# Decay rows of the first four blocks: small TensorE products and copies in place of a trip through DRAM

## The chip, the cores and the metric

One Trainium2 chip, one NeuronCore. The metric is the device time of one launch in microseconds. The kernel before has been run three times: 526.5, 527.76 and 527.88 us, median 527.76 us. One execution was also recorded by the hardware profiler; every duration below comes from that record, whose times count from the start of its span.

## What is computed

A gated linear recurrence over 768 steps (4 batches, 8 heads of 48), whose output goes through a feed-forward layer with a squared ReLU. q, k, v and alpha are float32; the two weight matrices arrive as 64-bit floats and are converted to float32 on the chip.

```python
def _attn_ref(q, k, v, alpha):
    for t in range(S):
        state = alpha[:, :, t, :, None] * state + einsum('bhd,bhe->bhde', k[:, :, t], v[:, :, t])
        y[:, :, t] = einsum('bhd,bhde->bhe', q[:, :, t], state)
...
h = np.maximum(x @ w_in, 0.0)      # x: 3072 x 384, w_in: 384 x 2048
return (h * h @ w_out)             # w_out: 2048 x 384
```

## The kernel before

The sequence is cut into chunks of 128 steps. A block is one chunk of one batch (all 8 heads), so there are 24 blocks, numbered chunk first: blocks 0 to 3 are the first chunk of the four batches. Four blocks make a group, whose 512 tokens go through the feed-forward layer together, so there are six groups.

For each block, `ln` takes the logarithm of alpha (L258), `cs` sums it along the chunk by one product with a triangular matrix (L280), and `eb` and `ei` make from the sums the decay `b` and its inverse `inv`, 128 steps by 384 (L291, L295). `mq` and `mk` scale q and k with them (L299). `qT` and `kT` turn q and k on TensorE (L336), `qc` and `kc` copy them to SBUF (L352). `sc` makes the scores and `kv` the sums of k times v in the same two PSUM banks (L399, L427); `am` masks the scores (L410); `us` adds the old state to the first half of kv (L440); `st` makes the next state: the second half of kv is added (L456) and the sum is scaled by the block's total decay (L457). `ya` and `yb` make the output of two blocks at once (L379, with a no-op on GpSimd between the two, L496), `ev` copies it into the layer's input `x` (L594).

The total decay is the last row of `b`, 384 numbers. L457 needs it as `last`, turned so that head and feature lie on the partitions: feature d of head 2p + e on partition 64 e + d, column p. Before, `bl` (L313) stores the row to DRAM (L317) and `br` (L319) loads it back in the turned layout with two DMAs of 192 numbers (L327). All DMAs are issued by SyncE in order. `st` runs for all but the last chunk, so 20 blocks need a `last`.

The tile `b` has two buffers, so block 3's `b` is written where block 0's stood once that has been read for `last`. All PSUM tiles share eight banks.

What runs before TensorE gets into the feed-forward layer is written out by hand: the word list `AT['first']` (L19) is walked at L948, and each word appends its step's instructions to the in-order queues of the engines. It holds everything for blocks 0 to 3, the words `ha0` to `ha3` and `hb0` to `hb3` (products of the feed-forward layer's first weights with the first half, blocks 0 and 1, and the second half of the group's tokens: L896, with ReLU and square on ScalarE, L902 and L905), and the conversion of the first three pieces of the 64-bit weights. One piece is converted by `first` on VectorE (L163, L167), `middle` on ScalarE (L177, L180) and `second` on VectorE (L188, L192, L195). `zeros` (L365) are products of zeros whose result nobody reads. What comes later (the other weights' conversion, the attention blocks 4 to 23) is woven into the feed-forward products by due times (`PLAN`, `EARLY`, `weave`), with `bl` and `br` for each of blocks 4 to 19.

The steps around the change run, by the word list, in this order:

```
... us0 bl1 qc1 kT1 ... br1 ei2 us1 ya0 eb2 yb0 zeros2 ln3 zeros2 mk2 load3k mq2 kT2 ev0 qT2 kc2 bl0 cs3
second0 qc2 eb3 first1 sc2 load3q kv2 ei3 mk3 load4q bl2 mq3 middle1 ha0 qT3 qc3 kT3 am2 kc3 weights6 second1
ha1 sc3 us2 load4k weights1 br2 br0 kv3 st0 bl3 ha2 am3 us3 load4v first2 ya2 weights3 br3 yb2 st3 ev2 middle2
ha3 hb3 second2 weights5 st2 hb0 weights4 load4a hb1 st1 hb2
```

Each engine takes only its own part of a word, so on VectorE us3 comes behind am3, that behind st0, and first2 behind us3.

## Time and profile before

| what | value |
|---|---|
| median of three runs | 527.76 us (526.5 to 527.88) |
| the profiled execution: its span, from the first to the last instruction (the page gives no other time of it) | 525.7 us |
| TensorE busy | 510.9 us, 97% of the span |
| VectorE busy | 363.8 us, 69% |
| ScalarE busy | 313.7 us, 60% |
| row stores (L317) | 20 of 1.5 KB, 0.24 to 0.78 us of issue each |
| loads of `last` (L327) | 40 of 0.8 KB, 0.33 to 2.80 us of issue each |
| waits for `last` (L457) | 8.6 us in 4 of 20 instructions |

A line of a timeline gives start, length, engine, line of the code, operation, output<-inputs, shapes and count, and in brackets the idle time of the engine ahead of it with what ended it. "PE y L379 <- DVE us L440: 4.0, 1, 4.0" in a list of waits reads: TensorE at L379 waited for VectorE's L440, 4.0 us in total, once, longest 4.0. The row PEclk of the page gives the TensorE clock that was granted in each of 40 slices of the span, in tenths.

### The profile page before, as it was taken

What the parts mean: (1) busy time and instruction counts of PE and PEld (TensorE: products, weight loads), DVE (VectorE), ACT (ScalarE), POOL (GpSimd) and SP (SyncE); (2) the same over time, 40 slices, a digit from 0 to 9 for tenths busy, and PEclk for the clock granted to TensorE, in tenths of its full rate; (3) what the DMA queues carried; (4) which work ended last, traced back from release to release, by engine and by line L of the source; (5) the groups of instructions that cost most, each with busy time, mean ns of one, the idle gap of its engine ahead of it and who ended that gap; (6) DMA issues with size and microseconds to landing.
All of it is one profiled execution on the core that took longest, in us unless ns stands there. A gap on an engine that the chain in (4) does not pass through costs nothing.

```text
span 525.7 us, 12899 instructions
## 1 busy us (share of the span) xinstructions
PE 510.9 (97%) x5276; PEld 421.6 (80%) x5276; DVE 363.8 (69%) x631; ACT 313.7 (60%) x654; POOL 5.3 (1%) x29
## 2 busy tenths in 40 slices
PE   6969999999999999999999999999999999999997
PEld 5656446567888769888899988899988899988997
DVE  4757978899879687865698365697365485363861
ACT  4638986588798576466963266963265773164620
POOL 4000000000000000000000000000000000000000
PEclk9888999999999999999999999999999999999999
DMA  9996877445488667898975697865774454798201
GB/s 190 191 262 137 237 200 200 106 93 211 153 235 232 151 192 188 246 357 225 252 189 187 218 281 183 214 175 175 224 251 150 153 156 138 240 362 287 87 0 60
DMA packets 140994, 102.34 MB, mean 195 GB/s; under 512 B 111476, under 2 KB 114568, under 8 KB 140936
## 3 DMA queue, kind: packets, MB, share of 16 engines
q1 hardware_dynamic: 140936, 101.53, 68.8%
q8 instruction: 41, 0.67, 0.6%
q14 instruction: 17, 0.14, 0.1%
HBM read 84.18 MB, written 17.33 MB: 193 GB/s over the span
## 4 chain that ended last, share of the span: by engine, by line
PE 76%; DVE 9%; ACT 7%; DMA 4%; issue 2%; SPq 2%; DVEq 0%; POOLq 0%
PE h L703 32%; PE o L786 32%; PE y L379 4%; ACT power L177 2%; PE T L556 2%; PE h L896 2%; PE sckv L399 2%; PE sckv L427 1%; SPq L119 1%; DVE w_out L192 1%; DVE w_out L195 1%; DMA wd<-do 1%; DMA v_in<-in_v_dram 1%; DVE wl L626 1%; DMA last<-row 1%
## 5 line engine op out<-in xcount | busy, mean ns | idle before, releaser
L703 PE MATMUL h<-xa,wb 128*128 128x512 f32 x240 | 68.8, 395 | 0.0
L703 PE MATMUL h<-xl,wl 128*128 128x512 f32 x240 | 67.8, 391 | 0.0
L703 PE MATMUL h<-xd,wd 128*128 128x512 f32 x240 | 66.6, 392 | 0.0
L594 ACT COPY x<-y 32x256 f32<-32x256 f32 (+2 forms) x132 | 47.3, 365 | 23.1 <-PE y L379 12.8
L720 ACT ACTIVATE h<-h 128x512 f32<-128x512 f32 x40 | 23.3, 581 | 59.9 <-PE h L703 59.7
L626 DVE TENSOR_TENSOR hid<-h,hid 128x512 f32<-128x512 f32 x40 | 27.5, 688 | 41.5 <-PE h L703 38.8
L786 PE MATMUL o<-wd,hd 128*128 128x384 f32 x304 | 54.4, 335 | 1.4 <-DVE osb L823 1.0
L786 PEld LDWEIGHTS o<-wd,hd 128*128 128x128 f32 x304 | 52.7, 188 | 2.4 <-DVE osb L823 1.4
L786 PE MATMUL o<-wb,ha 128*128 128x384 f32 x160 | 54.1, 338 | 0.0
L786 PE MATMUL o<-w_out,hid 128*128 128x384 f32 x160 | 53.5, 490 | 0.0
L786 PE MATMUL o<-wl,hl 128*128 128x384 f32 x160 | 53.5, 334 | 0.0
L703 PEld LDWEIGHTS h<-xl,wl 128*128 128x128 f32 x240 | 45.0, 188 | 10.0 <-DVE xl L626 0.3
L703 PEld LDWEIGHTS h<-xd,wd 128*128 128x128 f32 x240 | 44.6, 188 | 9.1
L703 PEld LDWEIGHTS h<-xa,wb 128*128 128x128 f32 x240 | 44.3, 188 | 9.2
L786 PE MATMUL o<-wb,hx 128*128 128x384 f32 x144 | 48.7, 338 | 0.0
L786 PE MATMUL o<-wl,hx 128*128 128x384 f32 x144 | 48.1, 334 | 0.0
L786 PEld LDWEIGHTS o<-w_out,hid 128*128 128x128 f32 x160 | 29.9, 190 | 19.7
L896 PE MATMUL h<-x,w_in 128*128 128x512 f32 (+1 forms) x120 | 44.8, 528 | 0.1
L676 ACT ACTIVATE ha<-hid 128x512 fp32r<-128x512 f32 x40 | 25.5, 636 | 23.8 <-DVE hx L626 13.0
L718 ACT ACTIVATE hid<-h 128x512 f32<-128x512 f32 x40 | 24.3, 607 | 25.2 <-PE h L703 25.1
L896 PEld LDWEIGHTS h<-x,w_in 128*128 128x128 f32 x120 | 23.7, 201 | 17.7 <-issue 14.4
L626 DVE TENSOR_TENSOR hl<-hid,ha 128x512 fp32r<-128x512 f32 x40 | 27.4, 685 | 11.6 <-ACT ha L676 11.6
(114 smaller groups left out, 878.3 us busy)
## 6 DMA issues: line engine op xcount, KB each, us to landing
wd<-do SPq DMA_DIRECT2D x36, 384.0 KB
wl<-lo SPq DMA_DIRECT2D x34, 384.0 KB
wl<-li SPq DMA_DIRECT2D x32, 384.0 KB
wd<-di SPq DMA_DIRECT2D x32, 384.0 KB
raw<-in_moe_w_in_dram SPq DMA_DIRECT2D x8, 768.0 KB
raw<-in_moe_w_out_dram SPq DMA_DIRECT2D x8, 768.0 KB
v_in<-in_v_dram SPq DMA_DIRECT2D x24, 192.0 KB
out_dram<-osb SPq DMA_DIRECT2D x24, 192.0 KB
```

The lines of the kernel that those rows point to most:

```text
L177: nc.scalar.activation(out=power, in_=power, func=AF.Relu, scale=2.0**23, bias=rebias)
L379: ins = nc.tensor.matmul(out=ys[e][64 * half : 64 * half + D + G * e, m % 2, p // 2, t], lhsT=lhsT, rhs=rhs, start=(half, e) not in seen, ...
L399: nc.tensor.matmul(out=ps[e][HALF[h], 0, p, :], lhsT=ks[rows, p, HALF[h]], rhs=qs[rows, p, HALF[h]], start=True, stop=True, skip_group_che ...
L556: nc.tensor.transpose(out=ps[h][:, i, p, :], in_=rows[HALF[h], 128 * p : 128 * (p + 1)], identity=ident[HALF[h], HALF[h]],)
L594: copy(out=x[kk][to : to + m, t : t + 2], in_=blk[n]["y"][e][r : r + m, :, p // 2],)
L626: nc.vector.tensor_tensor(out=o, in0=x, in1=z, op=op)
L676: nc.scalar.activation(out=a, in_=x, func=AF.Copy, scale=NEAR)
L703: nc.tensor.matmul(out=acc["h", j], lhsT=here[w, "i", p][:, kk, jj * 128 : (jj + 1) * 128], rhs=x_parts[x][:, kk], start=start and kk == 0 ...
L718: nc.scalar.activation(out=hid[j], in_=x, func=AF.Copy, scale=E)
L720: nc.scalar.activation(out=x, in_=x, func=AF.Copy, scale=1.0 + E)
L786: nc.tensor.matmul(out=acc[t][:, 0:DM], lhsT=lhs[:, t * C : (t + 1) * C], rhs=rhs, start=start, stop=stop, skip_group_check=True,)
L896: nc.tensor.matmul(out=ps, lhsT=w[:, kk, c0 : c0 + 128], rhs=xT[g][kk][:, cols], start=(kk == 0), stop=(kk == KM - 1),)
```

## The change

A new step `lt` takes the place of `bl` and `br` for blocks 0 to 3. Eight products, one for each head, take that head's 48 columns of `b` as the stationary operand and column 127 of the identity as the moving one, which picks row 127 of `b` and puts it on 48 partitions of a PSUM bank; two ScalarE copies of 48 partitions by 4 columns put the halves into `last`.

```diff
+    def lt(n):
+
+        ps = bank(n, "lastT")
+        for p in range(NP):
+            for e in range(2):
+                nc.tensor.matmul(
+                    out=ps[64 * e : 64 * e + D, 0, p : p + 1],
+                    lhsT=blk[n]["b"][:, (2 * p + e) * D : (2 * p + e + 1) * D],
+                    rhs=ident[:, C - 1 : C], start=True, stop=True, skip_group_check=True,
+                )
+        for e in range(2):
+            rows = slice(64 * e, 64 * e + D)
+            nc.scalar.copy(out=last_t[n % 4][rows, :], in_=ps[rows, 0, 0:NP])
+        given.add(("last", n))
...
-    steps = {f.__name__: f for f in (ln, sp, cs, eb, ei, mq, mk, bl, br, qT, qc, kT, kc, ev)}
+    steps = {f.__name__: f for f in (ln, sp, cs, eb, ei, mq, mk, bl, br, lt, qT, qc, kT, kc, ev)}
```

In the word list, lt1, lt0, lt2 and lt3 stand where bl1, bl0, bl2 and bl3 stood, and br0 to br3 are gone. The changed stretches of `AT['first']`:

```diff
-us0 bl1 qc1 ... weights2 br1 ei2 ... kc2 bl0 cs3 ... load4q bl2 mq3 ... weights1 br2 br0 kv3 st0 bl3 ha2 ... weights3 br3 yb2
+us0 lt1 qc1 ... weights2 ei2 ... kc2 lt0 cs3 ... load4q lt2 mq3 ... weights1 kv3 st0 lt3 ha2 ... weights3 yb2
```

Blocks 4 to 19 keep `bl` and `br`.

More of the change, by code (lines that the diff above doesn't have):

```diff
@@ L18 @@
 GB = 4
-AT = {'evs': 0.65, 'lead': 4, 'post': 3, 'w_first': (45.25, 42.0, 51.5), 'wstep': 1.6, 'w_in_at': 2.5, 'w_in_by': 3.4, 'room1': 22, 'room': 25, 's0': 4, 'ahead': 6, 'late': 2, 'xs': 0.2, 'g0': ((1.5, 4, False, True, 28.25), (20.25, 6, True, True), (28.75, 8, True, False)), 'sc0': (2.35, 2.35, 2.35), 'g1': ((5.5, 8, False, 15.5), (15.5, 10, True), (34.5, 12, True)), 'g': ((1.7, 6, True), (15.5, 8, True)), 'g1x': 50.0, 'gx': 48.25, 'g0x': 55.25, 'k0': 2, 'h0': 16, 'k1': 4, 'h1': 3, 'h1by': 2, 'evs0': 0.3, 'tp': 'ADMD', 'tp1': 'ADAD', 'split': 8, 'o0': (44.75, 47.25), 'o1': (), 'o2': (21.75, 27.5, 31.75, 35.0, 41.25, 41.75), 'str1': 22.0, 'ga': 9.5, 'gb': 13.0, 'cv0': 1.5, 'first': 'ln0 warm0 cs0 load0v ei0 mk0 kT0 eb0 mq0 qT0 ln1 kc0 qc0 cs1 load2a eb1 ei1 sc0 mq1 weights0 ln2 mk1 kv0 load1v am0 qT1 us0 bl1 qc1 kT1 first0 kc1 sc1 load2k middle0 load2q kv1 am1 load3a cs2 load3v load2v weights2 br1 ei2 us1 ya0 eb2 yb0 zeros2 ln3 zeros2 mk2 load3k mq2 kT2 ev0 qT2 kc2 bl0 cs3 second0 qc2 eb3 first1 sc2 load3q kv2 ei3 mk3 load4q bl2 mq3 middle1 ha0 qT3 qc3 kT3 am2 kc3 weights6 second1 ha1 sc3 us2 load4k weights1 br2 br0 kv3 st0 bl3 ha2 am3 us3 load4v first2 ya2 weights3 br3 yb2 st3 ev2 middle2 ha3 hb3 second2 weights5 st2 hb0 weights4 load4a hb1 st1 hb2'}
@@ new lines @@
+AT = {'evs': 0.65, 'lead': 4, 'post': 3, 'w_first': (45.25, 42.0, 51.5), 'wstep': 1.6, 'w_in_at': 2.5, 'w_in_by': 3.4, 'room1': 22, 'room': 25, 's0': 4, 'ahead': 6, 'late': 2, 'xs': 0.2, 'g0': ((1.5, 4, False, True, 28.25), (20.25, 6, True, True), (28.75, 8, True, False)), 'sc0': (2.35, 2.35, 2.35), 'g1': ((5.5, 8, False, 15.5), (15.5, 10, True), (34.5, 12, True)), 'g': ((1.7, 6, True), (15.5, 8, True)), 'g1x': 50.0, 'gx': 48.25, 'g0x': 55.25, 'k0': 2, 'h0': 16, 'k1': 4, 'h1': 3, 'h1by': 2, 'evs0': 0.3, 'tp': 'ADMD', 'tp1': 'ADAD', 'split': 8, 'o0': (44.75, 47.25), 'o1': (), 'o2': (21.75, 27.5, 31.75, 35.0, 41.25, 41.75), 'str1': 22.0, 'ga': 9.5, 'gb': 13.0, 'cv0': 1.5, 'first': 'ln0 warm0 cs0 load0v ei0 mk0 kT0 eb0 mq0 qT0 ln1 kc0 qc0 cs1 load2a eb1 ei1 sc0 mq1 weights0 ln2 mk1 kv0 load1v am0 qT1 us0 lt1 qc1 kT1 first0 kc1 sc1 load2k middle0 load2q kv1 am1 load3a cs2 load3v load2v weights2 ei2 us1 ya0 eb2 yb0 zeros2 ln3 zeros2 mk2 load3k mq2 kT2 ev0 qT2 kc2 lt0 cs3 second0 qc2 eb3 first1 sc2 load3q kv2 ei3 mk3 load4q lt2 mq3 middle1 ha0 qT3 qc3 kT3 am2 kc3 weights6 second1 ha1 sc3 us2 load4k weights1 kv3 st0 lt3 ha2 am3 us3 load4v first2 ya2 weights3 yb2 st3 ev2 middle2 ha3 hb3 second2 weights5 st2 hb0 weights4 load4a hb1 st1 hb2'}
```

## The prediction

> **What bounds the kernel now.** I read the page first: the span, the busy shares, the row of granted clock.

> ```profile
> span 525.7 us, 12899 instructions
> PE 510.9 (97%) x5276; PEld 421.6 (80%) x5276; DVE 363.8 (69%) x631; ACT 313.7 (60%) x654; POOL 5.3 (1%) x29
> PE   6969999999999999999999999999999999999997
> PEclk9888999999999999999999999999999999999999
> ```

> TensorE is busy from the fourth slice (39 us) to the end, so a gain must come from the first three slices, where it is not full and where its clock is below full. The edit lies there too: the hand-written order is over near 47 us. Second, the waits of TensorE between 30 and 135 us, and its timeline around the longest.

> ```profile
> PE y L379 <- DVE us L440: 4.0, 1, 4.0
> PE o L786 <- DVE osb L823: 1.0, 1, 1.0
> ```

> ```profile
> 30.22 1.53 PE L896 MATMUL h<-x,w_in 128*128 128x256 f32 x6
> 31.68 0.46 PE L379 MATMUL y<-qs,us 48*48 48x64 f32 x16
> 36.16 0.70 PE L379 MATMUL y<-qs,us 48*48 48x64 f32 x16 [4.02 <-DVE us L440]
> 36.62 2.37 PE L379 MATMUL y<-am,v_in 64*48 64x64 f32 x64
> ```

> One wait of 4.02 us stands in the middle of ya2: the products of block 3 need us3. Third, VectorE, which runs its instructions in order.

> ```profile
> 30.26 0.35 DVE L456 TENSOR_TENSOR s<-sckv,us 128x192 f32<-128x192 f32 x1
> 34.82 0.36 DVE L457 TENSOR_TENSOR s<-s,last 128x192 f32<-128x192 f32 x1 [4.22 <-DMA last<-row]
> 35.10 0.76 DVE L410 COPY_PREDICATED am<-halves_mask,sckv 128x256 f32<-128x256 uint32 x2
> 35.76 0.35 DVE L440 TENSOR_TENSOR us<-sckv,s 128x192 f32<-128x192 f32 x1
> ```

> us3 (35.76) is queued behind st0, which sits 4.22 us until block 0's decays have come back from DRAM. In the chain of waits the DMA that brings them is issued at 29.45 and takes 5.25 us. Fourth, windows of one microsecond, for the clock (columns: window, length, PE, PEld, DVE, ACT, POOL, granted clock, DMA share, GB/s).

> ```profile
> 34.00:35.00 1.00, 0.00 (x0) 0.00 (x0) 0.18 (x1) 0.00 (x0) 0.00 (x0) 1.00 0.70 166
> 36.00:37.00 1.00, 0.84 (x32) 0.84 (x36) 1.00 (x4) 0.00 (x0) 0.00 (x0) 0.50 1.09 274
> 42.00:43.00 1.00, 1.00 (x4) 0.81 (x3) 0.00 (x0) 0.97 (x3) 0.00 (x0) 0.68 0.00 0
> 43.00:44.00 1.00, 1.00 (x6) 0.89 (x5) 0.90 (x2) 0.97 (x3) 0.00 (x0) 1.00 0.02 8
> ```

> After the wait TensorE runs at half clock from 35.9 to 42.6 us. So the stall costs its own 4.02 us and then about half of the 6.5 us that follow. Last, the chain behind it:

> ```profile
> 47.52 0.39 ACT r L902
> 47.94 0.42 ACT hid L905
> 48.35 0.83 ACT power L177
> 130.46 3.07 PE o L786 x16
> ```

> From 47.5 to 130.5 us the chain runs on ScalarE and VectorE alone (the weights' conversion), and TensorE waits 1.0 us at its end. TensorE's own lead is therefore worth nothing by itself: what counts is how much earlier that conversion starts. From 131 us on TensorE has one wait of 0.4 us, so what is won by then is kept.

> **Removed.** On the DMA queue, four row stores (bl) and eight loads (br), 0.24 to 2.80 us of issue each. Loads behind them go out earlier. I count nothing for that: the DMA engines are full until 39 us, so bytes, not issues, set the landings. Raw weights stay early: by the landings in the trace piece 2 is in at 30.1 (needed at about 32), piece 3 at 33.9 (about 44), piece 4 at 37.4, piece 5 at 40.7. On VectorE, st0's 4.22 us and st3's 1.26 us go. The second is worth nothing, since ev2's copies wait for y2 then anyway. On ScalarE eb3's wait of 1.02 us for block 0's store goes; a wait for lt0 takes its place.

> **Added on TensorE.** Each lt has 8 products; an fp32 product is two instructions (L427's 16 are counted x32), so 16 with a 48-column load of all 128 rows and one moving column. No row shows that shape. Lower end: L399 at 23.52 to L427 at 24.04 is 32 instructions in 0.52 us, 16 ns each, 0.26 us per lt, in tiles that overlap. Upper end: kT, qT and cs start at 21.76, 22.20 and 22.63, 0.11 us for each transpose with its 128-column load, 1.76 us per lt. I take 48/128 of 0.11 us, 41 ns, **0.66 us per lt**, because the load sets the pitch of the nearest row with all 128 rows (the transpose). [...]

> **Added on ScalarE.** Two copies of 48x4 per lt. ACT L902 takes 380 ns for 256 columns and 596 ns for 512; the line through them leaves 165 ns at none. Upper end: 367 ns for the smallest copies (L594, 16x256). I take 0.2 us each, as the size falls off in the line.

> **The path, step by step.** lt1: between qT1 and kT1; its copies stand ahead of qc1 and kc1, so sc1 (12.75) moves about 1.1 us, to 13.9. kv1 waited until 14.30 for v anyway and goes to about 14.5: **+0.2 us**. lt0: between qT2 and cs3, from 22.63 to 23.3; the copies wait some 0.2 us for the last product to drain, 23.5 to 23.9, and qc2 runs behind them, 23.9 to 24.45. sc2 goes from 23.52 to 24.5, **+1.0**. eb3 ends near 25 instead of 24.98, so mk3 (25.56) is not later. lt2: **+0.66**. At qT3 TensorE waited 0.50 us for mq3, which swallows **0.50**. lt3: **+0.66**. So ya2 starts at 31.68 + 1.0 + 0.66 - 0.50 + 0.66 = 33.5. us3: kv3 ends at 31.4, masks 0.7, us3 0.35, so 32.4; no wait. y2 at full clock takes 1.41 + 0.62 us (the chain's pieces of the same products near 240 us) and 0.1 for the passing no-op: it ends at 35.65 instead of 38.97, **3.3 us earlier**.

> ev2, second2, st2 and st1 on VectorE follow with 3.3, so that first3 (L163, 47.16) starts at 43.8. ScalarE's middle3 (L177, 48.35) stood behind the copies of hb2. The 30 half products before it took 8.5 us, 3.7 of them at half clock; at 0.21 us each (256 columns of an L896 instruction) they take 6.4, plus about 1 us in which hb3 now waits for ev2. So they end at 43.0, hb2's copies at 43.9, first3's power at 44.3, and middle3 starts there: 48.35 - 44.3 = 4.05 us earlier. Less lt1's 0.2, **3.85 us**. The conversion, and TensorE at 130 us with it, keep that: span 525.7 - 3.85 = 521.85. The page gives no other time of that execution than its span; the median of the runs, 527.76, lies 2.06 us above it. With the same 2.06 around it the sum is **523.9 us**.

> What if covers fail: lt1's second copy is hidden only by v's landing (14.26), and costs up to 1 us without it; lt2 by qT3's 0.50.

> **Rivals.** (a) *The earlier dip goes too.* The clock also falls to 0.50 from 15.34 to 18.76, after a stretch (11.93 to 15.34) in which TensorE was busy 1.8 us of 3.41. Its falls and rises lie on one grid of 3.41 us. lt1 and the later kT1 raise that stretch to about 2.3 us, and the stretch from 5.10 to 8.51, with 2.2, was not followed by a fall. Then y0 ends about 1.4 us earlier, and VectorE's ev0 (idle 0.90 before 19.20) 0.9 earlier, bounded by raw piece 1 (23.91): 0.7 to 1.4 us more gain, 522.8. Against: the grid's phase is another in each execution. [...]

> (b) *The turns are dear but not ruinous.* At the transpose's 0.11 us each lt takes 1.76 us, 1.1 more: lt0, lt2, lt3 cost 3.3 us more, y2 ends at 38.9, and only the half products' clock is won, about 0.7 to 1.1 us: 526.8, within 0.3%. Half-way, at 1.2 us per lt, y2 gains 1.7 and the conversion about 2.4: 525.4. For: the load may not overlap. Against: every small product of the trace runs at 16 to 20 ns.

> (c) *They do not pipeline at all: slower.* The place is PE's queue between 22.6 and 32 us. If each instruction waits out its own load, 190 ns (PEld at L379, 64x48, mean 191), an lt takes 3.04 us, and y2 ends 3.9 us later than at 1.76: about 530.5. It decides from about 2.1 us per lt, 130 ns per instruction. Against: back-to-back loads in this trace, transposes included, never come so slowly.

> (d) *The wait stays elsewhere.* If the conversion did not start earlier, for example held by a raw piece, only the 1.0 us at 130 us would be won: 526.8. Against: the landings above.

> **How the numbers follow.** Forecast 523.9 (3 to 5 us gained) 0.45; (a) 0.20; half of (b) 0.13; (b) in full and (d) 0.14; (c) 0.08. A measurement of this kernel can tell about 0.3%, 1.6 us, from no change. Faster by more: 0.45 + 0.20 + 0.13 = 0.78; within: 0.14; slower: 0.08. The range runs from (a) with the copies and turns at their lower ends (0.4 us less per lt, three on the path, and a tenth for the copies: 521.5) to just short of (b) in full, 526.6.

> **What would show it.** Right: no wait of VectorE on last until 50 us; PE's ya2 in one run from about 33.5; granted clock 1.00 from 36 to 43 us; first3 near 43.8, middle3 near 44.3; PE o at 126.6 instead of 130.46. The 16 lt instructions show their pitch directly. Wrong: an lt above 1.2 us, a clock of 0.50 after 20 us, or a wait of ScalarE or VectorE on a raw piece or a bank between 40 and 130 us that was not there.

## The result, and the profile after

The changed kernel takes 530.76 us in the median of 14 runs (528.57 to 533.34), the kernel before 527.82 us of 14 (526.5 to 529.89) beside it: ratio 1.0053, 95% interval 1.0036 to 1.0069. By the medians it is 2.9 us slower, where 3.9 us less were forecast. The profiled execution of it took 528.85 us, with a span of 527.1 us.

First the page: span, TensorE's row, the clock.

```profile
span 527.1 us, 13013 instructions
PE   7899999899999999999999997999999999999997
PEclk9999999999999999999999998999999999999999
```

The first and third slices are fuller (7 and 9, where 6 and 6 stood), and the low clock of the first stage is gone. In the 25th slice (316 to 329 us) a new digit below 9 stands in both rows. Next VectorE around the stall that was to go:

```profile
30.47 0.35 DVE L471 TENSOR_TENSOR s<-sckv,us 128x192 f32<-128x192 f32 x1
30.93 0.36 DVE L472 TENSOR_TENSOR s<-s,last 128x192 f32<-128x192 f32 x1
31.86 0.35 DVE L455 TENSOR_TENSOR us<-sckv,s 128x192 f32<-128x192 f32 x1
```

It has gone: st0 runs through, and us3 starts at 31.86 instead of 35.76. Then the waits of TensorE for which nothing in the profile is the releaser ("issue"), up to 135 us and from there on; the kernel before has none.

```profile
PE y L394 <- issue: 1.9, 2, 1.5
```

```profile
PE y L394 <- issue: 2.7, 1, 2.7
```

The two long ones stand in the y products, in the middle of a row of equal instructions that need nothing new; this is the second, in TensorE's timeline and in windows of a microsecond:

```profile
317.36 0.54 PE L394 MATMUL y<-am,v_in 64*48 64x64 f32 x20
320.56 0.65 PE L394 MATMUL y<-am,v_in 64*48 64x64 f32 x11 [2.66 <-issue]
```

```profile
318.00:319.00 1.00, 0.00 (x0) 0.00 (x0) 1.00 (x4) 0.00 (x0) 0.00 (x0) 1.00 1.13 247
320.00:321.00 1.00, 0.44 (x11) 0.45 (x11) 0.63 (x2) 0.00 (x0) 0.00 (x0) 0.82 0.20 71
321.00:322.00 1.00, 1.00 (x6) 0.79 (x4) 0.00 (x0) 0.00 (x0) 0.00 (x0) 0.50 0.01 3
324.00:325.00 1.00, 1.00 (x6) 0.83 (x5) 0.00 (x0) 0.58 (x1) 0.00 (x0) 0.98 0.00 0
```

TensorE stands still from 317.9 to 320.6 us, and the clock is 0.50 for 3.4 us after it. Two marks of the chain of waits, the long rows of output products in the third and fourth group, tell what that cost; first after, then before:

```profile
269.02 29.32 PE o L801 x168
352.88 29.32 PE o L801 x168
```

```profile
272.22 29.32 PE o L786 x168
351.61 29.32 PE o L786 x168
```

At 269 us the changed kernel leads by 3.20 us; at 353 us it is 1.27 us behind. 4.47 us are lost between: 2.66 in the stop and some 1.7 in half of the 3.4 us at half clock.

**Theory F.** The page's DMA queues have one that carries instructions, 16 KB a packet:

```profile
q8 instruction: 42, 0.69, 0.5%
```

Before it had 41 packets and 0.67 MB. TensorE's part of the trace has 10685 instructions before and 10813 after. At 64 bytes for one, 16 KB are 256 of them, and the two programs 41.7 and 42.2 blocks, against 41 and 42 packets; the 64 bytes are inferred from that. Counted from 0 in the trace, the last instruction before the stop is number 7360 at 318 us, and 2240 at 102.8 us: 29 and 9 blocks, less 64 in both cases. (The same holds in the experiments below: each of the 24 stops of over 0.5 us after 40 us, in all traces, for which the profile names no releaser, stands behind a number 64 short of a multiple of 256.) The packet that ended the stop at 318 us ran from 317.99 to 318.87. So the theory: TensorE had used up its block and waited for the next. In sc, kv and ya it goes through 320 instructions in some 2.5 us, and if a block's ends lie so that all 256 are such small ones, the next block can come too late. The change adds 4 turns of 32 instructions (8 products, two passes, each a load and a matmul), 128 in all, and so moves every later block end by half a block against the bursts. **Theory E**, the rival: the loss comes from the early stage, or from transfers that now go at other times (the loads of last at 235 us, which the expectation below calls block 8's and which are those of blocks 14 and 15, end in a wait of 0.6 us of TensorE near 244 us).

### The profile page after: what moved, and what is told of

The parts are those of the page before. It is cut to its first block, busy times and chain, and to the rows that moved or that the text cites. A ratio compares the mean times of both kernels' runs of the same rounds, so it can differ in the third digit from the quotient of the medians.

```text
span 527.1 us, 13013 instructions
## 1 busy us (share of the span) xinstructions
PE 512.2 (97%) x5340; PEld 421.8 (80%) x5340; DVE 363.6 (69%) x631; ACT 314.9 (60%) x662; POOL 5.3 (1%) x29
## 4 chain that ended last, share of the span: by engine, by line
PE 87%; SPq 4%; DVE 3%; ACT 2%; DMA 2%; issue 1%; DVEq 0%; POOLq 0%; ACTq 0%
PE o L801 38%; PE h L718 31%; PE h L911 7%; PE y L394 4%; SPq L119 3%; PE T L571 2%; PE sckv L414 2%; PE sckv L442 2%; DMA raw<-in_moe_w_in_dram 1%; ACT x L609 1%; SPq L327 1%; DMA last<-row 1%; DVE wl L641 1%; PE cs L283 1%; PE cs L284 1%
## 5 line engine op out<-in xcount | busy, mean ns | idle before, releaser
L735 ACT ACTIVATE h<-h 128x512 f32<-128x512 f32 x40 | 23.3, 581 | 64.6 <-PE h L718 64.4
L718 PEld LDWEIGHTS h<-xl,wl 128*128 128x128 f32 x240 | 45.5, 189 | 10.2 <-DVE xl L641 0.3
L911 PE MATMUL h<-x,w_in 128*128 128x512 f32 (+1 forms) x120 | 43.6, 513 | 0.5 <-ACT x L609 0.5
L911 PEld LDWEIGHTS h<-x,w_in 128*128 128x128 f32 x120 | 22.1, 190 | 18.2 <-issue 13.9
```

The costliest lines, as they stand in the source:

```text
L718: nc.tensor.matmul(out=acc["h", j], lhsT=here[w, "i", p][:, kk, jj * 128 : (jj + 1) * 128], rhs=x_parts[x][:, kk], start=start and kk == 0 ...
L735: nc.scalar.activation(out=x, in_=x, func=AF.Copy, scale=1.0 + E)
L911: nc.tensor.matmul(out=ps, lhsT=w[:, kk, c0 : c0 + 128], rhs=xT[g][kk][:, cols], start=(kk == 0), stop=(kk == KM - 1),)
```

## The experiments

Where an experiment adds small products, it is this step (shortened here), with k as the number in the word:

```python
def pad(k):
    ps = bank(0, "pad")
    for i in range(k):
        nc.tensor.matmul(out=ps[64 * (i % 2) : 64 * (i % 2) + D, 0, 0:1], lhsT=ident[:, 0:D],
                         rhs=ident[:, C - 1 : C], start=True, stop=True, skip_group_check=True)
```

**1. The changed kernel, moved on to a whole block.**

```diff
-... load4a hb1 st1 hb2
+... load4a hb1 st1 hb2 pad32
```

> The changed kernel plus 32 products of 48x1 of the identity that nobody reads, at the end of the hand-written order (about 43 us, where TensorE has a lead over the weights' conversion). They are 128 TensorE instructions, so that with the 128 of the four turns every later instruction stands 256 further in the stream than in the kernel before: the same place in its 256-instruction block. Theory F (the loss is TensorE waiting for its own next block of instructions, because the change moved the block ends into the bursts of small products): no wait of over 1 us of TensorE that nothing in the profile explains after 60 us, no clock of 0.50 after 60 us, and 4 to 6 us less than the changed kernel: 525 to 527. Theory E (the loss comes from the early stage or from DMAs that now go at other times, as block 8's loads of last near 240 us): nothing is mended and 0.9 us of products is added, 530.8 to 531.7.

Measured: 525.56 us (523.15 to 527.21, 7 runs), before on that chip 527.51; ratio 0.9964 (0.9940 to 0.9987). From 60 us to the end these are TensorE's waits:

```profile
PE o L809 <- DVE osb L846: 0.8, 1, 0.8
PE o L809 <- DMA wd<-do: 0.4, 1, 0.4
```

No stop, no low clock after 60 us. The burst in which the changed kernel stood still now runs through:

```profile
317.85 0.68 PE L402 MATMUL y<-am,v_in 64*48 64x64 f32 x31
```

With products that nobody reads, the changed kernel is 0.4% faster than the one before.

**2. The kernel before, moved by half a block.** The same word in the kernel before.

> The kernel before plus the same 32 unread products at the same place: nothing else is changed, all row stores and loads stay. Every later TensorE instruction then stands in its block as in the changed kernel. Theory F: waits without a releaser appear in the y products near 106 and 321 us, 1.5 and 2.7 us long, the second with a clock of 0.50 behind it, and the time rises by 3 to 6 us over the kernel before, to 531 to 534. Theory E: 527.8 to 528.7, the price of the products at most.

Measured: 532.16 us (530.29 to 536.45, 7 runs); ratio 1.0096 (1.0063 to 1.0128). The stops are there, at 111.5 and at 326 us:

```profile
PE y L387 <- issue: 2.6, 2, 1.6
```

```profile
327.63 0.45 PE L387 MATMUL y<-am,v_in 64*48 64x64 f32 x12 [1.64 <-issue]
```

The second stands in the same place of the same burst as in the changed kernel (19 of the am products visible ahead of it, there 20), with the clock at 0.50 for 3.4 us behind it. None of the change is in this kernel, and it loses 4.6 us, of which the products' own time can be up to 1.4 us (see experiments 10 and 11). Theory E falls as the explanation of the loss.

**3 and 4. Other alignments.** The changed kernel with pad16 and with pad48.

> The changed kernel plus 16 unread products (64 instructions, half way between the two alignments). Theory F: block ends fall 64 instructions further into the bursts than in the changed kernel, the waits change in size or go elsewhere; the time is not the changed kernel's plus 0.45 us, it may lie anywhere from 524 to 533. Theory E: 530.8 to 531.3.

> The changed kernel plus 48 unread products (192 instructions, 64 beyond the alignment of the kernel before). Theory F: another set of waits, anywhere from 524 to 533, not a steady rise with the number of products. Theory E: 530.8 to 532.1, a steady rise of 0.45 us for each 16 products at most.

Measured: 534.30 us with 16 (ratio 1.0123, 1.0091 to 1.0154), 527.87 us with 48 (1.0010, 0.9989 to 1.0030). No steady rise: the time goes 530.8, 534.3, 525.6, 527.9 us with 0, 16, 32 and 48. With 16 a stop of 2.8 us stands at 238.8 us, with the clock at 0.50 for 6.8 us behind it, and one of 2.0 us in the output products at 269.9 us, with 3.4 us at 0.50. The profile puts the second down to VectorE, but it too stands behind an instruction 64 short of a multiple of 256, and ends 1.3 us after a packet. With 48 there are two stops, 1.1 us at 174.9 and 0.6 at 207.5. But the 48 products cost more than their own time where they stand: the clock is 0.50 from 45.5 to 48.9 us behind them, and ScalarE waits for the products that follow, which holds the weights' conversion:

```profile
49.95 0.60 ACT L925 ACTIVATE r<-h 128x512 f32<-128x512 f32 x1 [2.39 <-PE h L919]
```

With 32 it has no such wait. So the four times mix two things; experiment 7 takes them apart.

**5. The same TensorE time in 8 instructions.**

```diff
+    def big(_):
+        ps = bank(0, "big", (2 * NP, 64))
+        for _ in range(2):
+            nc.tensor.matmul(out=ps[:, 0:NP, :], lhsT=s_t[3].rearrange("a p d -> a (p d)")[:, 0:128],
+                             rhs=s_t[3], start=True, stop=True)
...
-... hb1 st1 hb2
+... hb1 st1 hb2 big0
```

> The changed kernel plus two unread products of 128x256 at the end of the hand-written order: 0.85 us of TensorE time, as the 32 small ones, but only 8 instructions. Theory F (place in the 256-instruction blocks): the alignment stays the changed kernel's within 8 instructions, the unexplained waits near 102 and 318 us stay, 530 to 533 us. Rival T (what mended the changed kernel was the extra TensorE time at that place, by moving its work against the transfers): 525 to 526.5, as with the 32 small products.

Measured: 528.80 us (525.79 to 530.80, 10 runs), before 528.22; ratio 1.0006 (0.9983 to 1.0030). The number lies between the two and fits neither. The profile bears out F in kind: the stops are at their old places, 103 and 318 us, with one more at 399 and one of 0.8 us in the output products at 346. In that execution they were short (0.9 us at most) and no low clock followed. Time alone does not mend the kernel as the 32 small ones do; how far the 2 us below my figure are the 8 instructions or chance was asked again in experiment 12.

**6. The products only ahead of the second stop.**

```diff
 units.append((0, begun, (g,)))
+if g == 2:
+    units.append((0, pad, (3, 2)))
```

The 3 and the 2 are the digits of 32.

> The changed kernel plus the 32 unread products at the start of the third group (about 217 us), behind the wait at 102 us and ahead of that at 318 us. Theory F: the wait of 1.5 us at 102 stays and costs nothing, since TensorE waits for the weights' conversion at 126 us anyway; that at 318 us goes, and its clock of 0.50 with it. The time is the one with the products at 43 us plus the 0.9 us that they cost in a stage without slack: 525.5 to 527.5. Rival T: no gain at all, 530.8 to 532.

Measured: 525.07 us (524.54 to 526.56, 5 runs), before 528.22; ratio 0.9955 (0.9934 to 0.9975). The stop at 102 us is still there, 1.3 us; that at 318 us is gone. The expectation that the first one is free was wrong in part: see below.

**7. A whole block more.** The changed kernel with pad64.

> The changed kernel plus 64 unread products, 256 instructions: one whole block, so the alignment is the changed kernel's again. Theory F: the waits near 102 and 318 us come back, 530.5 to 533 us, though twice as many products were added as in the version that mended it. Rival T and any theory in which the products help by their time: not slower than 528.

Measured: 531.96 us (529.70 to 533.84, 5 runs); ratio 1.0082 (1.0052 to 1.0112). The stops are back, 1.4 and 1.0 us in the y products near 107 and 321 us, and 0.9 us in the output products at 350. Not all of the loss against experiment 1 is theirs: behind the 64 products the clock is 0.50 for 3.4 us, ScalarE waits 2.7 us, and the output product behind the conversion starts at 130.6 us instead of 127.4. What comes after that product is free of this. From it to the end of the span:

| kernel | us |
|---|---|
| before | 395.2 |
| changed, two executions (result, experiment 12) | 400.0, 397.4 |
| changed with 16, 32, 48, 64 products | 404.4, 395.5, 396.8, 398.4 |
| before with 32 products | 399.4 |

32 products mend this stretch and 64 do not: what counts there is the number of instructions modulo 256.

**8. One turn alone.** lt0 as in the changed kernel, blocks 1 to 3 with their bl and br, and 56 products for the alignment.

```diff
-us0 lt1 qc1 ... weights2 ei2 ... load4q lt2 mq3 ... weights1 kv3 st0 lt3 ha2 ... weights3 yb2 ... hb2
+us0 bl1 qc1 ... weights2 br1 ei2 ... load4q bl2 mq3 ... weights1 br2 kv3 st0 bl3 ha2 ... weights3 br3 yb2 ... hb2 pad56
```

> Only block 0's row is turned on TensorE; blocks 1, 2 and 3 keep the store and the loads. 56 unread products (224 instructions) with the 32 of the one turn bring the stream to the alignment of the kernel before. My theory of the gain: st0's wait of 4.22 us is the only one of the four that holds TensorE; so this has the whole gain of the four turns and 0.45 us per turn less TensorE time before 33 us: 524.5 to 526, no later than the fully changed kernel at the same alignment (525.6). Rival: the other blocks' loads behind it in the DMA queue hold st3, st2 or the raw weights, and the gain shrinks: 526.5 to 528.

Measured: 531.22 us (531.04 to 531.85, 4 runs); ratio 1.0071 (1.0053 to 1.0088). My theory of the gain fails here. The rival's mechanism is there, but its range (526.5 to 528) is missed too. VectorE:

```profile
37.79 0.36 DVE L480 TENSOR_TENSOR s<-s,last 128x192 f32<-128x192 f32 x1 [4.20 <-DMA last<-row]
```

```profile
PE h L919 <- ACT x L617: 3.7, 1, 3.7
```

With st0's wait gone, st3 waits 4.20 us for block 3's row, ev2's copies stand behind it, and TensorE waits 3.7 us for them in hb3, with the clock at 0.50 from 38.7 to 45.5 us. The wait is handed from the first row to the last: block 3's turn is needed beside block 0's, and whether the two suffice was not run. The time itself is not the price of the missing turns alone: first3 is still 0.9 us earlier than in the kernel before (46.30 against 47.16). That is lost behind the 56 products, where ScalarE waits 2.1 us: the last L163 is 3.1 us later (110.99 against 107.91).

**9. The disputed cost by itself.**

```diff
+    def burst(_):
+        ps = [bank(0, "burst") for _ in range(2)]
+        for i in range(256):
+            h, e = i % 2, i // 2 % 2
+            nc.tensor.matmul(out=ps[h][64 * e : 64 * e + D, 0, 0:64], lhsT=ident[HALF[h], 0:D],
+                             rhs=ident[HALF[h], 0:64], start=True, stop=True, skip_group_check=True)
```

> The changed kernel plus two bursts that nobody reads: 256 products of 64x48 by 64x64 in four tiles of the array (1024 TensorE instructions, four blocks), one at the start of the fifth group, with the other transfers under way, one behind the last output product, with few of them left. It measures the disputed cost by itself. Theory F: such products run at 7 to 8 ns per instruction, so a block lasts some 2 us, and TensorE stops at each block's end, every 256 instructions, with one fetch of 16 KB on the instruction queue for each stop; from the start of a block to the start of the next 4 to 5 us with the transfers, somewhat less without. If fetches keep ahead, the 1024 instructions run through in about 8 us with no stop over 0.3 us, and theory F falls.

This is the burst behind the last output product, in TensorE's timeline (a line is a run of matmuls; as many loads go with them):

```profile
537.81 1.84 PE L348 MATMUL burst<-ident 64*48 64x64 f32 x116
541.23 2.00 PE L348 MATMUL burst<-ident 64*48 64x64 f32 x128 [1.59 <-issue]
544.69 2.00 PE L348 MATMUL burst<-ident 64*48 64x64 f32 x128 [1.45 <-issue]
548.14 1.10 PE L348 MATMUL burst<-ident 64*48 64x64 f32 x60 [1.45 <-issue]
```

128 matmuls with 128 loads, a stop, 128 with 128, a stop: a block takes 3.46 us from start to start (541.23, 544.69, 548.14), and 2.0 of them are work. (The program was run once, under the profiler.) Its packet on the instruction queue starts 1.14 us after the block, runs 0.96, and the next block starts 1.36 us after its end (541.23, 542.37 to 543.33, 544.69). In the fifth group, with transfers under way, the blocks start at 386.21, 390.76 and 394.49: 4.55 and 3.73 us.

```profile
386.21 2.00 PE L348 MATMUL burst<-ident 64*48 64x64 f32 x128 [1.41 <-issue]
390.76 3.40 PE L348 MATMUL burst<-ident 64*48 64x64 f32 x128 [2.55 <-issue]
394.49 0.32 PE L348 MATMUL burst<-ident 64*48 64x64 f32 x5 [0.33 <-issue]
```

(The block from 390.76 ran at half clock, so its work took 3.4 us, and a wait of 0.33 us still followed.) So **in a row of small products, a block that is worked off in less than about 3.5 to 4.6 us makes TensorE wait for the rest**. The y bursts go through one in about 2 us.

A lone short block need not stop: in the kernel before, one of 1.86 us from 263.77 passes without a wait, since a packet had run ahead of it, from 262.16 to 263.52. What decides is when the packet lands. In all fourteen traces TensorE stands still for over 0.25 us at the end of a block 31 times, and each time it goes on 1.2 to 1.8 us after the end of a packet. What starts a packet early or late stays open.

**10 and 11. Both kernels with the blocks out of the bursts.** The trace of experiment 6 gives the time of every 256 successive instructions for each alignment; 23 products at 43 us and 21 at 217 us leave none under 4.2 us after 45 us. In the kernel before 55 and 21 give the same places.

> The changed kernel with 23 unread products at the end of the hand-written order and 21 at the start of the third group. The two numbers are chosen from the trace of an earlier experiment so that, by its times, no block of 256 instructions lasts less than 4.2 us after 45 us. Theory F: no unexplained wait over 0.7 us after 60 us, and the best time of the series, 524 to 525.5, 0.6 us of added products in it. If the alignment were not the cause: 530.8 and up.

> The kernel before, with all its stores and loads, brought by 55 and 21 unread products to the same places in the blocks as the changed kernel with 23 and 21 (that is 32 products, the four turns' instructions, more at 43 us). Against that kernel it gives the change alone, with the alignment the same on both sides. My working, mended only for the blocks: 3 to 4 us slower than it, 527 to 528.8. If the gain of the four turns were itself small: less than 1.5 us apart.

Measured: the changed kernel 524.65 us (523.55 to 526.90, 7 runs), before 527.30 unpadded; ratio 0.9956 (0.9939 to 0.9974). The kernel before, padded, 529.79 us (528.72 to 532.41, 6 runs); ratio 1.0058 (1.0037 to 1.0079). From 60 us on the first has one wait of TensorE:

```profile
PE o L809 <- DVE osb L846: 0.9, 1, 0.9
```

In both TensorE has no stop without a releaser after 60 us. They are 5.1 us apart. The unread products cost more than I had reckoned: 32 of them are 64 matmuls, from 42.8 to 44.2 us in the profile of experiment 1, 1.4 us instead of 0.9. The kernel before has 32 more of them; without their 1.4 us, if none of it is hidden, the change alone is worth 3.7 us at equal alignment, against the 3.85 worked out. (In the profiles the stretch from first3 to the last L163 is 1.9 us longer with the 55 products, 62.6 against 60.7 us, and 0.7 longer with the 23, 61.2 against 60.5; with that 1.2 it is 3.9 us.) The same mistake fits the padded kernel before being 1 us slower than expected: 76 products take 3.3 us, not 2.1.

**12. The changed kernel again.**

> The changed kernel once more, on the same chip as the three others. Theory F gives what was measured, 530.8 (529 to 532), since nothing in the program moves; the version with two large products, 8 instructions away, came out 2 us lower than I expected, and this tells whether that was the chip or the 8 instructions: near 528.8 here, it was the chip.

Measured: 529.75 us (525.43 to 533.78, 12 runs); ratio 1.0042 (1.0015 to 1.0068), 5.1 us over experiment 10 on the same chip. Its granted clock was 0.999 in the two shortest runs (525.43, 526.00) and 0.987 to 0.990 in three long ones (532.36 to 532.82), but 0.990 in one of 529.68 too. The profiled execution, 526.00 us, has both stops (3.9 us in all) and no low clock. So the spread goes in the main with the clock; that the low clock of the long runs lay behind the stops is likely and not shown, since they were not profiled. Experiment 5's 528.8 lies within the spread; whether its 8 instructions did anything stays open.

## Why the prediction was wrong

**The step that failed** is this one: "From 131 us on TensorE has one wait of 0.4 us, so what is won by then is kept." It took the later stages as they were in the trace before. But the change adds 128 instructions to TensorE's program, and every later instruction gets another place in its 256-instruction block. The 3.20 us by which it still led at 269 us were more than lost in one stop at a block's end and the low clock behind it. None of the rivals was this: I priced the added instructions by their time and not by their place.

**What was right.** The mechanism that was to save time worked as worked out, and up to 104 us a little better (times in us, predicted from the working, measured in the profile after):

| mark | before | predicted | after |
|---|---|---|---|
| us3 | 35.76 | 32.05 | 31.86 |
| end of y2 | 38.97 | 35.65 | 34.7 |
| first3 | 47.16 | 43.8 | 42.86 |
| middle3 | 48.35 | 44.3 | 43.45 |
| last L163 on VectorE | 107.91 | 104.06 | 103.38 |
| PE o behind the conversion | 130.46 | 126.6 | 127.05 |

The terms: a turn costs TensorE 0.46 us (22.48 to 22.94), not 0.66. Its matmuls start in pairs: 6 ns apart within a pair and 45 ns from pair to pair, so 22 ns each on average, near the lower end. I had taken 41 ns for each, which is nearly what a pair takes; that the load sets the pitch was my estimate from the transposes, and no run shows it. The 16 loads of a turn start 21 ns apart on average, and the record of each lasts 119 to 125 ns, so here they overlap. The two copies take 0.32 us, where 0.4 was taken. The clock stays at 1.00 from 36 to 43 us.

**What was wrong besides.** *TensorE's lead before 130 us is worth nothing*: not quite. The lead of the conversion is 4.53 us up to 103 us and 3.41 at 127. Between them ScalarE, which copies y for the layer, waited for the stopped y products:

```profile
ACT x L609 <- PE y L394: 1.2, 1, 1.2
```

So the stop at 102.8 us cost 1.1 us, although TensorE itself had time in hand. The other profiles agree: from the last L163 to that output product it is 22.5 to 22.6 us in the seven without a stop in these y products and 23.1 to 24.1 us in the seven with one. *st3's wait is worth nothing, since ev2's copies wait for y2 anyway*: in experiment 8 y2 is early, and st3's 4.20 us hold TensorE for 3.7. The sum was right only because lt3 goes with lt0.

**Rival (a)**, the dip at 15 us: it is absent in the profile after, as (a) had it, but the change did not remove it. The phase of the grid does differ between the two profiles: the falls at 15.34 us before and 320.63 us after lie 1.69 and 3.22 us past whole steps of 3.413 us. Of the ten profiles of the changed kernel, as it is or with products added, four have a clock of 0.50 that begins between 12.2 and 15.1 us, and six have none; of the three of the kernel before, two have it. Without it middle3 starts at 42.5 to 43.7 us in the changed kernel, with it at 43.9 to 45.2. So most of the 0.9 us by which first3 and middle3 beat the forecast, about what (a) priced, was the luck of that execution. **(b) and (c)**, dear turns, fell with the 0.46 us. **(d)** fell with the table.

The best of the versions measured are the changed kernel with its blocks out of the bursts (experiment 10, ratio 0.9956 to the kernel before) and that of experiment 6 (0.9955), where the change as it stands has 1.0053.

## What to carry to other kernels

Added instructions have a place as well as a price (here 128 of them went with 2.9 us more, and 128 unread ones on top brought the kernel to 0.4% under the one before): before you trust a saving of a few microseconds, count the instructions that it adds or takes on TensorE, and look where that moves the block ends in its later bursts of small ones. If a change that wins in its own stage loses at the end, look for waits without a releaser and for the packets of the instruction queue beside them, then shift the program by a known number of idle instructions and see whether the loss moves; count what those instructions cost where they stand. When a wait on one of several like transfers goes, ask which of the others is then the last.

## What the runs showed of the hardware

The clock fell to 0.50 after a stop of 2.66 us in one execution of the changed kernel, and after one of 2.4 us in another execution it did not; in experiment 2 it fell after one of 1.64 us. In the trace before the falls (15.34, 35.82) and rises (18.75, 42.65) keep to a grid of 3.41 us, and in that after the clock is low for one such step, from 320.63 to 324.05. In the step ahead of a fall TensorE was busy 1.80 and 0.00 us before, and 0.75 us after; in the step of the stop at 102.8 us (102.17 to 105.59) it was busy 1.92 us, and no fall followed. Whether that decides it, no run tests. So one stop had two prices, and runs of one program spread: 525.4 to 532.8 us in experiment 12, against 523.6 to 526.9 for experiment 10, which has no stops.
